# Attention and top-80 expert routing on one core: the expert lists in exact bf16 parts, list one-hots on VectorE, two thirds of the band masks off TensorE, one PSUM ring of four

## The chip, the cores and the metric

The program runs on one core of a Trainium2 chip. The metric is the device time of one execution in microseconds (us). Engines are named as in the profile: PE is TensorE (PEld its weight loads), DVE VectorE, ACT ScalarE, POOL GpSimd, SP SyncE; SP and POOL also issue the DMAs.

## The reference

For 8 batches and 8 heads, 32 global and 512 local tokens of 64 dimensions attend: global tokens to everything, local tokens to the 32 global keys and to a band of 32 positions to either side. The 4608 rows of 512 that come out go through a gate with eight experts, of which each keeps the 80 tokens with the largest gate weight.

```python
s_g = scale * q_g @ k_all.T;  out_g = softmax(s_g) @ v_all
s_ll = where(abs(i - j) <= 32, scale * q_l @ k_l.T, -1e9)
out_l = softmax(concat([scale * q_l @ k_g.T, s_ll])) @ concat([v_g, v_l])
x = concat([out_g, out_l])                       # rows of 512
logits = x @ w_gate;  expert = argmax(logits);  gate_w = softmax(logits)[expert]
for e in range(8):                               # capacity 80
    tok = the 80 tokens of expert e with the largest gate_w
    out[tok] = gate_w[tok] * (relu(x[tok] @ w1[e]) @ w2[e])
```

## The kernel before

The main loop has 16 stages, s = 0 to 15, one for each half of a batch's heads (four heads, k = 0 to 3, in two pairs j). A stage computes on PE: `G_val(s)` and `L_val(s, k)`, which multiply the exponentials of the scores (`eG`, `eL`) by the values (`vgb` global, `vt` local) into `o_ps`; `S_glob(s+1)` and `S_loc(s+1, j)`, the scores of the next stage, whose exponentials ACT takes; `T_tile`, the transposes of queries and keys to come; `X_turn`, which turns the normalised output `xn` for the gate; and `O_glob`, the global queries. In `S_loc` the band mask is made in one of two ways for each head, by the table `MASKER`: "pe" adds a matrix of large negative numbers by one more matmul before the scores (L264, 128x512, bf16), "dve" or "pool" multiplies the exponentials by 0 or 1 afterwards (L277).

In `G_val` every head has 32 rows of the array: four matmuls of 32 rows and 65 columns for each quarter u of the tokens. An fp32 matmul stands in the profile as two records (80 of L473 for 8 batches of 5 matmuls).

After a batch's second stage `gate_pieces(b)` hands a list of small steps to a queue, `bgq`. The loop pops ten of them in each stage, by calls `bg(1)`, `bg(1)`, `bg(1)`, `bg(1)`, `bg(1)`, `bg(2)`, `bg(3)` between the attention's parts. Each engine runs its instructions in the order in which the program is written (the schedule is manual). The steps of a batch are

- `p_xg`, `p_lgT`, `p_lg`, `p_arg`: logits (first by four groups of 512 tokens, then turned back by eight-column matmuls with `sel`, L379), argmax one-hot `oh` and gate weight;
- `p_parts`, `p_turn0`, `p_vi`, `p_turn1`, `p_glob`, five `p_rank`: the gate weight is split into three bf16 parts on POOL; matmuls and VectorE counts (L457) give each token's rank in its expert, by comparison with all tokens of its batch;
- `p_oh`, `p_list`: five one-hots `ohs` of the ranks on POOL (L466) and five fp32 matmuls (L473) put the first 80 values and ids of the batch into `B_ps`; the batch's list is merged with the list so far, `Rl`;
- for batches 1 to 6 `p_diag`, two `p_cmp`, `p_oh2`, `p_sort`: the merged list `M` is sorted again. POOL spreads the values on a diagonal, four fp32 matmuls of 320 columns (L494, L496) make all differences, DVE compares and counts, POOL makes eight one-hots (L506), eight fp32 matmuls (L512) permute.

That is 16 steps for batches 0 and 7 and 21 for batches 1 to 6, against 20 that two stages pop. What is left when the loop ends is run by `bg(100)`; then the indices `idx` are made, the tokens gathered (POOL, indirect DMA), and the eight experts run, each with a scatter to the output from POOL. The weights of experts 6 and 7 are loaded only after the first gathers.

PSUM: `psT` tiles come from a ring T of two banks, `psS` tiles (scores) from a ring S of two, `o_ps` from two double banks.

## Time and profile before

| | |
|---|---|
| runs | 435.69, 431.42, 428.17 us, median 431.42 |
| profiled execution | 427.29 us, its span 425.5 us |
| busy in the span | PE 323.1 us (76%), DVE 160.3 (38%), ACT 116.5 (27%), POOL 159.3 (37%) |
| granted TensorE clock | 0.755 of 2.4 GHz over the span |
| DMA | 51.35 MB, software queue 38.1% and hardware queue 19.5% of the engines' span |

A profile row gives line, engine, operation, output<-inputs, shapes and count, then busy us and the mean ns of one, then the idle time of the engine before it and what released it. The granted clock is given in the windows as PEclk (1.00 is 2.4 GHz, 0.50 is 1.2 GHz).

### The profile page before, as it was taken

The page shows a single profiled execution, that of the slowest core. Times are in us where ns is not written, and L with a number is a line of the kernel's source. Part 1 is how long each engine was busy: PE and PEld are TensorE (multiplying, and loading weights), DVE is VectorE, ACT ScalarE, POOL GpSimd, SP SyncE. Part 2 cuts the span into 40 slices and gives each one's busy share as a digit, 9 for nine tenths or more (in the row PEclk, how much of TensorE's full clock was granted, in tenths as well). Part 3 has the DMA queues.
Part 4 walks back from the last instruction along what each step waited for, and adds up shares of the span by engine and source line. Part 5 has one row for each costly group of instructions (what it writes and reads, how often), then busy time and mean ns, then how long its engine had stood idle before and what let it go on. Part 6 is the DMA issues. An engine that isn't in the chain of part 4 may idle for free. (4 is left out here: it accounts for less than half of the span.)

```text
span 425.5 us, 10554 instructions
## 1 busy us (share of the span) xinstructions
PE 323.1 (76%) x4528; PEld 223.3 (52%) x4528; DVE 160.3 (38%) x422; ACT 116.5 (27%) x181; POOL 159.3 (37%) x301
## 2 busy tenths in 40 slices
...
GB/s 153 176 224 91 198 240 225 166 99 161 160 29 103 161 164 126 28 169 157 102 24 104 101 75 151 100 101 61 193 2 146 53 201 0 2 148 216 127 46 46
DMA packets 61790, 51.35 MB, mean 121 GB/s; under 512 B 45360, under 2 KB 45488, under 8 KB 61744
## 3 DMA queue, kind: packets, MB, share of 16 engines
q0 software_dynamic: 18000, 27.66, 38.1%
q1 hardware_dynamic: 43744, 23.03, 19.5%
...
q14 instruction: 11, 0.09, 0.1%
...
## 5 line engine op out<-in xcount | busy, mean ns | idle before, releaser
L298 PE MATMUL o_ps<-vt,eL 128*64 128x65 f32 x1024 | 53.7, 266 | 0.0
L115 ACT COPY qkT<-T_ps 128x1024 f16<-128x1024 f16 x29 | 29.3, 1011 | 73.9 <-PE T_ps L230 71.2
L298 PEld LDWEIGHTS o_ps<-vt,eL 128*64 128x64 f32 x1024 | 44.9, 173 | 8.5 <-issue 5.4
L342 POOL CAST xb<-xn 128x1024 bf16<-128x1024 f32 x16 | 16.6, 1035 | 74.0 <-DVE xn L305 62.1
L274 ACT ACTIVATE eL<-l_ps 128x512 f32<-128x512 f32 x64 | 34.8, 596 | 31.0 <-PE l_ps L269 30.7
L230 PE MATMUL T_ps<-ident,qk 128*64 128x128 f16 x512 | 26.8, 268 | 16.2 <-DMA qk<-in_q_l_dram 9.5
L506 POOL TENSOR_SCALAR oh<-second,rs 80x80 f32<-80x80 bf16 x48 | 22.1, 473 | 40.1 <-DVE rs L501 32.6
L457 DVE SCALAR_TENSOR_TENSOR junk<-r_ps,gate,second 128x512 bf16<-128x512 f32 x40 | 29.9, 747 | 13.5 <-PE r_ps L456 12.4
L230 PEld LDWEIGHTS <-qk 128*64 128x64 f16 x512 | 22.8, 144 | 20.0 <-DMA qk<-in_q_l_dram 9.5
L466 POOL TENSOR_SCALAR ohs<-second,rank 128x80 f32<-128x80 bf16 x40 | 19.0, 484 | 34.7 <-DVE rank L464 34.7
L289 PE MATMUL o_ps<-vgb,eG 32*128 32x65 f32 x512 | 27.5, 367 | 0.0
L289 PEld LDWEIGHTS o_ps<-vgb,eG 32*128 32x128 f32 x512 | 24.8, 274 | 4.2 <-issue 4.1
L473 PE MATMUL B_ps<-vi,ohs 128*80 128x24 f32 (+1 forms) x80 | 16.9, 299 | 12.7 <-POOL ohs L466 11.6
L337 PE MATMUL x_ps<-identf,xn 128*128 128x128 f32 x128 | 25.3, 331 | 0.5 <-DVE junk L457 0.5
L250 ACT ACTIVATE eG<-G_ps 128x512 f32<-128x512 f32 x16 | 9.5, 596 | 59.0 <-PE G_ps L248 59.0
L473 PEld LDWEIGHTS B_ps<-vi,ohs 128*80 128x80 f32 (+1 forms) x80 | 12.6, 213 | 20.2 <-POOL ohs L466 17.6
L305 DVE TENSOR_TENSOR xn<-o_ps,rec 128x512 f32<-128x512 f32 x32 | 22.1, 692 | 2.1
L277 DVE TENSOR_TENSOR eL<-eL,first 128x512 f32<-128x512 f32 x16 | 11.1, 692 | 31.3 <-ACT eL L274 31.3
L115 DVE COPY xT<-x_ps 128x512 f32<-128x512 f32 x32 | 21.9, 683 | 1.4 <-PE x_ps L337 1.2
...
L456 PE MATMUL r_ps<-S3T,oh3T 24*128 24x512 bf16 x40 | 17.7, 442 | 5.0 <-DVE junk L457 2.1
L264 PE MATMUL l_ps<-first 128*128 128x512 bf16 x48 | 18.5, 440 | 1.8 <-ACT eG L250 1.1
...
## 6 DMA issues: line engine op xcount, KB each, us to landing
...
```

Source lines behind the costliest of these rows:

```text
L115: (nc.scalar.copy if eng is nc.scalar else eng.tensor_copy)(out=out, in_=in_)
L230: nc.tensor.transpose(out=T_ps[64 * q:64 * q + 64, i, :], in_=qk16[b % 2][:, t, q, 8 * half + i, :], identity=ident16[:, :])
L264: mm(out=l_ps[hh][:], lhsT=identb, rhs=neg, start=True, stop=False, skip_group_check=True)
L274: nc.scalar.activation(out=e, in_=l_ps[hh][:], func=AF.Exp, scale=scale)
L289: mm(out=oview(s, k)[:, u, :], lhsT=eG[s % 2][r, 128 * u:128 * u + 128], rhs=vgb[r, s // 2, s % 2, :], start=(u == 0), stop=False, skip_gr ...
L298: mm(out=o[64 * odd:64 * odd + 64, u, :], lhsT=eL[s % 2][:, k, 64 * t:64 * t + 64], rhs=v[:, 4 * odd + u, k, :], start=False, stop=(u == 3 ...
L305: nc.vector.tensor_tensor(out=xn[:, s % 2, :, j].rearrange("p u h d -> p h u d"), in0=o[:, :, :, 0:64], in1=rec[:].unsqueeze(3).to_broadca ...
L337: nc.tensor.transpose(out=x_ps[:, 128 * u:128 * u + 128], in_=xn[:, s % 2, u, j].rearrange("p h d -> p (h d)"), identity=identf[:, :])
L457: nc.vector.scalar_tensor_tensor(out=junk[:], in0=ps_[:], scalar=st["gate"][:, u:u + 1], in1=wst[:, 512 - 128 * u:1024 - 128 * u], op0=ALU ...
L466: nc.gpsimd.tensor_scalar(out=ohs[:, u, :], in0=nat if b == 0 else rev, scalar1=rank[:, u:u + 1], scalar2=None, op0=ALU.is_equal)
L473: mm(out=B_ps[:].rearrange("r e c -> r (e c)"), lhsT=ohs[0:n, u, :], rhs=st["vi"][0:n, u].rearrange("p e c -> p (e c)"), start=(u == 0), s ...
L506: nc.gpsimd.tensor_scalar(out=oh2[:, e, :], in0=nat[0:cap], scalar1=st["rs"][:, e:e + 1], scalar2=None, op0=ALU.is_equal)
```

## The change

- `MASKER` goes from pe, pe, pe, dve to pool, pe, dve, pool: one mask matmul a stage in place of three, and two multiplications on POOL, one on DVE.
- `G_val`: the global values `vgb` are laid out with the two heads of a pair block-diagonally, so that one matmul of 64 rows and 130 columns does what two of 32 rows and 65 columns did.
- Logits by token quarters: sixteen matmuls of 128 columns that add up the four head groups in PSUM, and one fp32 transpose in place of the four `sel` matmuls. ACT's copy is 128x128 instead of 128x512.
- The value is carried as three bf16 parts and each id as two, seven columns `vi` in place of three in fp32. The matmuls of `p_list`, `p_cmp` and `p_sort` become bf16: 5 of 56 columns, 24 of 80, 8 of 7. `p_diag` is gone, so the list has 20 steps for batches 1 to 6.
- `ohs` and `oh2` are made by one DVE instruction each, the comparison by eight DVE counts (L495 after), the `oh3` copy moves to ACT, and so does the copy of `X_turn(s, 1)`.
- `psT` and `psS` share one ring of four banks.
- `vgb` is cleared in parts at the start (eight memsets on DVE, one before), the `cid` load is part of `second`.

```diff
-MASKER = ["pe", "pe", "pe", "dve"]
+MASKER = ["pool", "pe", "dve", "pool"]
...
     def psT(shape, dt, name):
-        return ps.tile(shape, dt, tag="T", bufs=2, name=name)
+        return ps.tile(shape, dt, tag="S", bufs=4, name=name)
 
     def psS(name):
-        return ps.tile([P, 512], FP32, tag="S", bufs=2, name=name)
+        return psT([P, 512], FP32, name)
...
-    vgb = cp.tile([P, B, 2, 65], FP32, name="vgb")
+    vgb = cp.tile([P, B, 2, 2, 65], FP32, name="vgb")
...
-    ohs = cp.tile([P, 5, cap], FP32, name="ohs")
+    lgT = cp.tile([P, P], FP32, name="lgT")
+    Rl = cp.tile([cap, 8, 7], BF16, name="Rl")
+    Rv = cp.tile([cap, 8], FP32, name="Rv")
+    oh2 = cp.tile([cap, 8, cap], BF16, name="oh2")
+    ohs = cp.tile([P, 5, cap], BF16, name="ohs")
...
-    def oview(s, k):
-        return ost[s][k // 2][:, k % 2, 0:260].rearrange("p (u d) -> p u d", u=4)
+    def oview(s, k, u):
+        c = 130 * (u % 2) + 65 * (k % 2)
+        return ost[s][k // 2][:, u // 2, c:c + 65]
 
     def G_val(s):
         ost[s] = [psO(f"o_ps{s}_{j}") for j in range(2)]
         for u in range(4):
-            for k in range(4):
-                r = slice(32 * k, 32 * k + 32)
-                mm(out=oview(s, k)[:, u, :], lhsT=eG[s % 2][r, 128 * u:128 * u + 128],
-                   rhs=vgb[r, s // 2, s % 2, :], start=(u == 0), stop=False, skip_group_check=True)
+            for j in range(2):
+                r = slice(64 * j, 64 * j + 64)
+                c = 130 * (u % 2)
+                mm(out=ost[s][j][:, u // 2, c:c + 130], lhsT=eG[s % 2][r, 128 * u:128 * u + 128],
+                   rhs=vgb[r, s // 2, s % 2].rearrange("p h d -> p (h d)"), start=(u % 2 == 0), stop=False,
+                   skip_group_check=True)
...
         def p_lgT():
-            ps_ = psT([P, 512], FP32, f"lgT_ps{b}")
+            ps_ = psT([P, P], FP32, f"lgT_ps{b}")
             for f in range(4):
-                mm(out=ps_[32 * f:32 * f + 32, :], lhsT=wg[:, f, :], rhs=xslot(2 * b + f // 2, f % 2)[:],
-                   start=True, stop=True, skip_group_check=True)
+                for c in range(4):
+                    mm(out=ps_[32 * c:32 * c + 32, :], lhsT=wg[:, f, :],
+                       rhs=xslot(2 * b + f // 2, f % 2)[:, 128 * c:128 * c + 128],
+                       start=(f == 0), stop=(f == 3), skip_group_check=True)
             nc.scalar.copy(out=lgT[:], in_=ps_[:])
 
         def p_lg():
-            lg = psT([P, 5, E], FP32, f"lg{b}")
-            for u in range(4):
-                mm(out=lg[:, u, :], lhsT=lgT[:, 128 * u:128 * u + 128], rhs=sel[:], start=(u == 0), stop=False,
-                   skip_group_check=True)
-            mm(out=lg[:, 4, :], lhsT=identb, rhs=zb[:], start=False, stop=False, skip_group_check=True)
+            lg_ps = psT([P, 5, 32], FP32, f"lg{b}")
+            lg = lg_ps[:, :, 0:8]
+            nc.tensor.transpose(out=lg_ps[:, 0:4, :].rearrange("p u e -> p (u e)"), in_=lgT[:], identity=identf[:, :])
+            mm(out=lg[:, 4, :], lhsT=identb, rhs=zb[:], start=True, stop=False, skip_group_check=True)
...
+            nc.vector.tensor_tensor(out=t("sc", [P, 5, E])[:], in0=st["oh"][:],
+                                    in1=st["gate"][:].unsqueeze(2).to_broadcast([P, 5, E]), op=ALU.mult)
+            nc.scalar.copy(out=t("oh3", [P, 5, 3, E], BF16)[:], in_=st["oh"][:].unsqueeze(2).to_broadcast([P, 5, 3, E]))
...
         def p_vi():
-            oh, g, vi = st["oh"], nc.gpsimd, st["vi"]
-            g.tensor_copy(out=vi[:, :, :, 0], in_=st["sc"][:])
-            for c in range(2):
-                g.tensor_tensor(out=vi[:, :, :, 1 + c], in0=oh[:],
-                                in1=cid[:, b, :, c].unsqueeze(2).to_broadcast([P, 5, E]), op=ALU.mult)
+            nc.gpsimd.tensor_tensor(out=st["vi"][:, :, 3:7, :], in0=st["oh"][:].unsqueeze(2).to_broadcast([P, 5, 4, E]),
+                                    in1=cid[:, b].unsqueeze(3).to_broadcast([P, 5, 4, E]), op=ALU.mult)
...
         def p_oh():
             rank = t("rank", [P, 5])
             nc.vector.tensor_tensor(out=rank[:], in0=st["rk1"][:], in1=st["rk2"][:], op=ALU.add)
-            for u in range(5):
-                nc.gpsimd.tensor_scalar(out=ohs[:, u, :], in0=nat if b == 0 else rev, scalar1=rank[:, u:u + 1],
-                                        scalar2=None, op0=ALU.is_equal)
+            nc.vector.tensor_tensor(out=ohs[:], in0=(nat if b == 0 else rev).unsqueeze(1).to_broadcast([P, 5, cap]),
+                                    in1=rank[:].unsqueeze(2).to_broadcast([P, 5, cap]), op=ALU.is_equal)
 
         def p_list():
-            B_ps = psT([cap, 8, 3], FP32, f"B_ps{b}")
+            B_ps = psT([cap, 8, 7], FP32, f"B_ps{b}")
             for u in range(5):
                 n = P if u < 4 else SG
-                mm(out=B_ps[:].rearrange("r e c -> r (e c)"), lhsT=ohs[0:n, u, :],
-                   rhs=st["vi"][0:n, u].rearrange("p e c -> p (e c)"), start=(u == 0), stop=(u == 4))
+                mm(out=B_ps[:], lhsT=ohs[0:n, u, :], rhs=st["vi"][0:n, u].rearrange("p c e -> p e c"),
...
+            M = t("M", [cap, 8, 7], BF16)
+            bv = t("bv", [cap, 8])
+            mv = t("mv", [cap, 8])
+            mask = t("mask", [cap, 8, 7], U8)
+            nc.scalar.copy(out=M[:], in_=B_ps[:])
+            nc.vector.tensor_reduce(out=bv[:], in_=B_ps[:, :, 0:3], axis=AX.X, op=ALU.add)
+            nc.vector.tensor_tensor(out=mask[:], in0=Rv[:].unsqueeze(2).to_broadcast([cap, 8, 7]),
+                                    in1=bv[:].unsqueeze(2).to_broadcast([cap, 8, 7]), op=ALU.is_ge)
             nc.vector.copy_predicated(out=M[:], mask=mask[:], data=Rl[:])
...
+            nc.vector.tensor_tensor(out=mv[:], in0=Rv[:], in1=bv[:], op=ALU.max)
+            fin["M"], fin["mv"] = M, mv
 
         def p_cmp(h):
             def f():
-                es = slice(4 * h, 4 * h + 4)
                 D_ps = psT([cap, 4, cap], FP32, f"D_ps{b}_{h}")
-                mm(out=D_ps[:].rearrange("i e k -> i (e k)"), lhsT=negones[:],
-                   rhs=mdiag[:, es].rearrange("k e i -> k (e i)"), start=True, stop=False)
-                mm(out=D_ps[:].rearrange("i e k -> i (e k)"), lhsT=identf[0:cap, 0:cap],
-                   rhs=st["M"][:, es, 0:1].to_broadcast([cap, 4, cap]), start=False, stop=True)
-                nc.vector.tensor_tensor(out=gt2[:, es], in0=D_ps[:],
...
-                if h == 1:
-                    nc.vector.tensor_reduce(out=t("rs", [cap, 8])[:], in_=gt2[:], axis=AX.X, op=ALU.add)
+                if h == 0:
+                    t("rs", [cap, 8])
+                for e in range(4 * h, 4 * h + 4):
+                    for c in range(3):
+                        mm(out=D_ps[:, e % 4, :], lhsT=st["M"][:, e, c:c + 1].to_broadcast([cap, cap]),
+                           rhs=identb[0:cap, 0:cap], start=(e % 4 == 0 and c == 0), stop=(c == 2),
+                           skip_group_check=True)
+                for e in range(4 * h, 4 * h + 4):
+                    nc.vector.scalar_tensor_tensor(out=junk[0:cap, 0:cap], in0=D_ps[:, e % 4, :],
+                                                   scalar=st["mv"][:, e:e + 1], in1=w80, op0=ALU.subtract,
+                                                   op1=ALU.is_gt, accum_out=st["rs"][:, e:e + 1])
...
         def p_oh2():
-            for e in range(8):
-                nc.gpsimd.tensor_scalar(out=oh2[:, e, :], in0=nat[0:cap], scalar1=st["rs"][:, e:e + 1],
-                                        scalar2=None, op0=ALU.is_equal)
+            nc.vector.tensor_tensor(out=oh2[:], in0=nat[0:cap].unsqueeze(1).to_broadcast([cap, 8, cap]),
+                                    in1=st["rs"][:].unsqueeze(2).to_broadcast([cap, 8, cap]), op=ALU.is_equal)
...
         def p_sort():
-            R_ps = psT([cap, 8, 3], FP32, f"R_ps{b}")
+            R_ps = psT([cap, 8, 7], FP32, f"R_ps{b}")
             for e in range(8):
                 mm(out=R_ps[:, e, :], lhsT=oh2[:, e, :], rhs=st["M"][:, e, :], start=(e == 0), stop=(e == 7),
                    skip_group_check=True)
-            nc.vector.tensor_copy(out=Rl[:], in_=R_ps[:])
+            nc.scalar.copy(out=Rl[:], in_=R_ps[:])
+            nc.vector.tensor_reduce(out=Rv[:], in_=R_ps[:, :, 0:3], axis=AX.X, op=ALU.add)
...
-            ls += [p_diag, p_cmp(0), p_cmp(1), p_oh2, p_sort]
+            ls += [p_cmp(0), p_cmp(1), p_oh2, p_sort]
...
+    for k in range(4):
+        r = slice(32 * k, 32 * k + 32)
+        nc.vector.memset(vgb[r, :, :, 1 - k % 2, :], 0.0)
+        nc.vector.memset(vgb[r, :, :, k % 2, 64:65], 1.0)
...
-        X_turn(s, 1, nc.vector)
+        X_turn(s, 1, nc.scalar)
...
-        nc.vector.tensor_scalar(out=idx[:, c, :], in0=M[:, :, 1 + c], scalar1=BIG, scalar2=None, op0=ALU.add)
+        nc.vector.scalar_tensor_tensor(out=idx[:, c, :], in0=M[:, :, 3 + 2 * c], scalar=BIG,
+                                       in1=M[:, :, 4 + 2 * c], op0=ALU.add, op1=ALU.add)
```

The list steps on PE at the end of the last stage, program before: `x_ps_1` is that stage's second `X_turn`, `B_ps`, `D_ps` and `R_ps` belong to batch 6, `xgT_ps` is the first step of batch 7.

```order
L337 MATMUL x_ps_1_4309<-identf,xn 128x128 x4
L456 LDWEIGHTS oh3T
L456 MATMUL r_ps_3_4315<-S3T,oh3T 128x512
...
L456 MATMUL r_ps_4_4318<-S3T,oh3T 128x512
L473 MATMUL B_ps_4338<-vi_4172,ohs 80x24 x5
L494 MATMUL D_ps_0_4350<-mdiag,negones 80x320
L496 MATMUL D_ps_0_4350<-M_4344,identf 80x320
L494 MATMUL D_ps_1_4354<-mdiag,negones 80x320
L496 MATMUL D_ps_1_4354<-M_4344,identf 80x320
L512 MATMUL R_ps_4368<-M_4344,oh_110 80x3 x8
L366 MATMUL xgT_ps_4378<-identf,xgn_4091 128x128
```

The same place on PE now (rows of a tile that follow one another alike are left out):

```order
L450 MATMUL r_ps_4_4282<-S3T,oh3T 128x512
L336 MATMUL x_ps_0_4285<-identf,xn 128x128 x4
L316 MATMUL og_4291<-vt_82,eQ_90 32x65 x16
L321 MATMUL og_4291<-vgb,egg 32x65 x4
L466 LDWEIGHTS ohs
L466 MATMUL B_ps_4319<-vi_4158,ohs 80x56
...
L491 MATMUL D_ps_0_4334<-first,M_4325 80x80
...
L336 MATMUL x_ps_1_4352<-identf,xn 128x128 x4
...
L491 MATMUL D_ps_1_4358<-first,M_4325 80x80
...
L507 MATMUL R_ps_4376<-M_4325,oh_107 80x7
...
L365 MATMUL xgT_ps_4397<-identf,xgn_4153 128x128
```

Before, batch 6's last two rank steps and its whole list stood behind the attention of the last stage; now they are spread over that stage, and batch 7's steps follow its second `X_turn` and the sort.

DVE at the end of a batch's list, program before (batch 6):

```order
L464 TENSOR_TENSOR rank_4321<-rk_4299,rk_4266 128x5
L480 COPY M_4344<-B_ps_4338 80x24
L481 TENSOR_TENSOR mask_4345<-Rl,M_4344 80x24
L483 COPY_PREDICATED M_4344<-mask_4345,Rl 80x24
L498 TENSOR_TENSOR gt_111<-D_ps_0_4350,second 80x320
L498 TENSOR_TENSOR gt_111<-D_ps_1_4354,second 80x320
L501 TENSOR_REDUCE rs_4358<-gt_111 80x8
L514 COPY Rl<-R_ps_4368 80x24
```

And now:

```order
L458 TENSOR_TENSOR rank_4316<-rk_4218,rk_4216 128x5
L459 TENSOR_TENSOR ohs<-second,rank_4316 128x400
L477 TENSOR_REDUCE bv_4326<-B_ps_4319 80x8
L478 TENSOR_TENSOR mask_4328<-Rv,bv_4326 80x56
L480 COPY_PREDICATED M_4325<-mask_4328,Rl 80x56
L481 TENSOR_TENSOR mv_4327<-Rv,bv_4326 80x8
L495 SCALAR_TENSOR_TENSOR junk,rs_4335<-D_ps_0_4334,mv_4327,second 80x80 x4
L495 SCALAR_TENSOR_TENSOR junk,rs_4335<-D_ps_1_4358,mv_4327,second 80x80 x4
L501 TENSOR_TENSOR oh_107<-second,rs_4335 80x640
L510 TENSOR_REDUCE Rv<-R_ps_4376 80x8
```

Both sets of one-hots and the counts stand on DVE now; in the stages that compute scores the mask multiplication of head 2 stands between the two groups of four counts.

## Rows read from the trace of the kernel before

**Rows 1.** Windows: us, busy us of each engine, PEclk, DMA share, GB/s.

```profile
32.20:50.80 18.60, 17.42 (x444) 13.59 (x442) 8.35 (x18) 11.41 (x18) 7.94 (x12) 1.00 0.68 138
50.80:83.80 33.00, 28.29 (x500) 20.41 (x498) 16.09 (x43) 14.37 (x22) 12.90 (x26) 0.84 0.94 213
83.80:295.60 211.80, 182.07 (x2553) 125.78 (x2552) 86.57 (x240) 68.47 (x105) 78.95 (x158) 0.73 0.49 110
295.60:333.60 38.00, 32.35 (x406) 22.48 (x405) 17.56 (x48) 5.66 (x10) 13.30 (x28) 0.68 0.46 99
333.60:348.50 14.90, 10.04 (x34) 6.16 (x35) 2.33 (x6) 0.00 (x0) 8.55 (x16) 0.50 0.84 153
348.50:371.50 23.00, 11.64 (x58) 5.94 (x58) 10.34 (x30) 1.42 (x3) 7.86 (x21) 0.50 0.09 17
371.50:425.50 54.00, 28.81 (x352) 19.49 (x352) 11.76 (x24) 3.50 (x8) 19.68 (x22) 0.82 0.56 115
```

**Rows 2.** Groups by line: busy, mean ns of one, idle before them.

```profile
L274 ACT ACTIVATE eL<-l_ps 128x512 f32<-128x512 f32 x64 | 34.8, 596 | 31.0 <-PE l_ps L269 30.7
L457 DVE SCALAR_TENSOR_TENSOR junk<-r_ps,gate,second 128x512 bf16<-128x512 f32 x40 | 29.9, 747 | 13.5 <-PE r_ps L456 12.4
L264 PE MATMUL l_ps<-first 128*128 128x512 bf16 x48 | 18.5, 440 | 1.8 <-ACT eG L250 1.1 <-ACT eL L274 0.7
L473 PE MATMUL B_ps<-vi,ohs 128*80 128x24 f32 (+1 forms) x80 | 16.9, 299 | 12.7 <-POOL ohs L466 11.6
L512 PE MATMUL R_ps<-M,oh 80*80 80x3 f32 x96 | 14.1, 246 | 5.2 <-POOL oh L506 4.9
L277 DVE TENSOR_TENSOR eL<-eL,first 128x512 f32<-128x512 f32 x16 | 11.1, 692 | 31.3 <-ACT eL L274 31.3
L379 PE MATMUL lg<-sel,lgT 128*128 128x8 f32 x64 | 9.9, 282 | 1.7 <-ACT lgT L374 1.6
L487 POOL TENSOR_TENSOR mdiag<-identf,M 80x640 f32<-80x640 f32 x6 | 7.6, 1265 | 5.1 <-DVE M L483 5.1
L393 DVE SCALAR_TENSOR_TENSOR key<-sh,second 128x40 f32<-128x40 f32 x8 | 1.6, 195 | 0.1
```

**Rows 3.** Timeline of `G_val` at either clock: start, us, instructions.

```profile
41.16 1.12 PE L289 MATMUL o_ps<-vgb,eG 32*128 32x65 f32 x32
...
123.29 1.99 PE L289 MATMUL o_ps<-vgb,eG 32*128 32x65 f32 x32
```

**Rows 4.** Timeline of the sort's differences, matmuls and one weight load.

```profile
118.81 1.35 PE L494 MATMUL D_ps<-mdiag,negones 80*80 80x320 f32 x2
...
119.95 1.27 PE L496 MATMUL D_ps<-M,identf 80*80 80x320 f32 x2
119.95 0.26 PEld L496 LDWEIGHTS D_ps<-M,identf 80*80 80x80 f32 x1 [0.28 <-issue]
```

**Rows 5.** Timeline of the experts' bf16 matmuls of 80 columns, at either clock.

```profile
375.14 1.23 PE L721 MATMUL h_ps<-eQ,wr 128*128 128x80 bf16 x16 [0.42 <-DVE eQ L712]
...
389.95 0.74 PE L721 MATMUL h_ps<-eQ,qk 128*128 128x80 bf16 x16
```

**Rows 6.** Timeline around 60 us: POOL and DVE together, a wait for PSUM.

```profile
60.21 1.04 POOL L342 CAST xb<-xn 128x1024 bf16<-128x1024 f32 x1 [0.40 <-DVE key L393]
...
60.45 0.85 DVE L398 TENSOR_TENSOR oh<-key,m 128x40 f32<-128x40 f32 x1
...
62.26 0.64 PE L230 MATMUL T_ps<-ident,qk 128*64 128x128 f16 x16 [1.74 <-DVE xT L115]
```

**Rows 7.** Timeline of the end of batch 7's list.

```profile
364.59 2.33 POOL L466 TENSOR_SCALAR ohs<-second,rank 128x80 f32<-128x80 bf16 x5 [6.87 <-DVE rank L464]
...
366.87 3.77 POOL L681 MEMSET xT<- 80x512 bf16 x8
367.47 0.18 DVE L480 COPY M<-B_ps 80x24 f32<-80x24 f32 x1 [3.04 <-PE B_ps L473]
...
368.11 2.56 DVE L679 TENSOR_SCALAR idx<-M 80x8 uint32<-80x8 f32 x2
...
371.55 1.10 POOL L684 DMA_INDIRECT xT<-x_scr,idx  x1 [0.91 <-POOL xT L681]
```

96 lines of the change are left out of this document (35 added, 61 removed).

## The prediction, made before the changed kernel ran

> **What bounds the kernel.** I read the windows first, cut by the starts of `G_val`, then the groups by line, then the timeline. In the windows [rows 1] PE is busy 17.4 of 18.6 us in stages 0 and 1, 182 of 211.8 in stages 4 to 13; from stage 2 on no engine but PE and its loads passes 49% (ACT 61% before that; the DMA share is 0.94 in stages 2 and 3, 0.49 afterwards). So PE's static order is the bound of the loop. Two things make a stage pair, 18.6 us without gate steps, into 42.4 us (211.8 / 5): some 9.5 us of gate matmuls and 5 us of waits, and the clock, 1.00 in the first window and 0.73 later, which is 1.2 GHz for (1 - 0.73) / 0.5 = 54% of the time. The same 32 records take 1.12 us at 2.4 GHz and 1.99 at 1.2 [rows 3], a factor of 1.77. Check: (18.6 + 9.5) us of full-clock work at a rate of 0.46 + 0.54 / 1.77 = 0.765 is 36.7, and 5 of waits make 41.7.
>
> After the loop 14.9 and 23.0 us [rows 1], together 37.9, are a chain of small steps: the list of batch 6 left in the queue (21 steps a batch, 20 popped), then all of batch 7. The last 54.0 us (experts, weights 6 and 7, scatters) start with the first gather and are not touched; I take them as they are.
>
> **The sum, part by part.** Per batch, that is per pair of stages, PE time:
>
> - Masks: 32 of the 48 matmuls of L264 go, 18.5 / 48 = 0.385 us each [rows 2], four a pair: -1.5. In their place POOL gets 32 multiplications: 1.265 us for 640 columns [rows 2], so 1.0 for 512, 32 us in all, while it loses 40 + 48 one-hots and the diagonals; DVE keeps its one. The first is wanted by `L_val(s+1, 0)` half a stage later, the other by `L_val(s+1, 3)` later still, so PE hides them. Queued behind them on POOL are `shift_v`, `X_cast` and the DMA issues, each with more than 1 us to spare. If that cover failed, at most 1 us a stage, 16 us in all.
> - Logits: L379 is (9.9 + 1.7) / 8 = 1.45 us a batch [rows 2]; one 128-column transpose, at the 0.28 of one such record, replaces it: -1.2. The sixteen quarter matmuls stream as many columns as the four did: 0.
> - List: L473 is (16.9 + 12.7) / 8 = 3.7 us, paced by POOL's one-hots. Five bf16 matmuls at the pace of L721 (0.74 / 16 = 0.046 us, or 1.23 / 16 = 0.077 [rows 5]) are 0.3. A new wait stands before them: DVE must finish a count (0.75), a copy, `rg`, `xgn`, `rank` and the one-hot (692 x 400 / 512 = 0.54 us [rows 2]), against `X_turn`, `O_glob` and `T_tile` on PE: about 1.2 left. So -2.2.
> - Differences: four fp32 matmuls are eight records at 0.55 us ((119.95 - 118.81) / 2 [rows 4]), 4.4 at 1.2 GHz, half at 2.4, about 3.5 in the mix. Now 24 x 0.046 to 0.077 = 1.1 to 1.85, plus 0.8 for the merged list (an ACT copy, mask, predicated copy) directly behind the list on PE: -1.2.
> - Sort: L512 was (14.1 + 5.2) / 6 = 3.2 us. Now 0.5, and a wait: from the end of the first differences DVE needs four counts, the mask of head 2, four counts and `oh2`. A count of 80 columns lies between 0.20 (40 columns, L393) and 0.75 (512, L457 [rows 2]); I take 0.4 with its accumulator read, near the small one: 1.6 + 0.7 + 1.6 + 692 x 640 / 512 = 0.87, together 4.8, of which `S_loc`, `X_turn` and the second differences on PE cover 1.7. So 0.5 + 3.1: +0.4 (bounds -1 and +3).
> - The ring of four takes away waits like the 1.74 us of `T_ps` on a copy two tiles back [rows 6], and `oh3` comes from ACT instead of a late POOL: -1.5 together (0 to -3). Against it, `X_turn(s, 1)` on ACT stands between two exponentials and the copy that `p_glob` waits for; L274's 0.596 us has its shape [rows 2]: +0.6.
> - `G_val`: eight groups of four records at 0.111 us become eight of two with twice the columns. From below half of that (-0.9 a pair), from above twice (+1.8 at 2.4 GHz). I take +0.5, nearer to zero, because in rows 4 the load of the next weights (0.26 us) fits wholly inside the running matmul of the same rows (0.55).
>
> Sum of a pair: -1.5 - 1.2 - 2.2 - 1.2 + 0.4 - 1.5 + 0.6 + 0.5 = -6.1. Six such pairs (batches 1 to 6) give -36.6, batch 0 (no sort) -5.3, stages 0 and 1 -1.2: -43. The same number of waits in shorter, denser stages should give a little clock back; from 54% at 1.2 GHz to 49% is worth 0.6 us a pair, -4. **Loop: -47.**
>
> **Tail:** the 14.9 us of batch 6's list go, since its 20 steps now end with the loop (its cost is in the pairs). In batch 7's chain the logits save 1.5. The one-hots and list go from 3.0 us (364.5 to 367.4 [rows 7]) to 1.2: -1.8. The indices took 2.56 us for two instructions of 80x8 while POOL's memsets ran, and the gather followed those memsets; without `ohs` in front on POOL they are over before: -2.5. **Tail: -21.**
>
> At nothing: the memsets of `vgb` (about 4 us more on DVE at the start; PE's first work waited until 9.5 us for queries) and the dropped `cid` load, both hidden by loads.
>
> 427.3 - 47 - 21 = **359 us**, against the profiled execution's own 427.3; the median of the runs is 431.4, 1% more, which the range takes in. A kernel like this cannot be told from no change within 2%, 8.6 us.
>
> **A rule against it.** The Trainium skill, "TensorE: Matmul & The Clock Gate", Part 3, says that a weight load overlaps running matmuls only where the row group differs. The new `G_val` has two row groups where it had four, so by that rule load and stream would add up. Rows 4 show the contrary for 80 rows, so I keep +0.5; no row shows 64-row pairs. A second rule, "SBUF — State Buffer", section "Who interferes with whom", says that a DVE instruction with two SBUF inputs and a GpSimd one that reads SBUF lock each other out. By it the 32 masks would hold up the one-hots on DVE.
>
> **Rivals.**
> 1. *`G_val` twice as long.* Load and stream in series: 0.111 us more in 16 x 8 groups is 14 us at 2.4 GHz, 25 at 1.2, 20 in the mix. For it: 130 columns of fp32. Against: rows 4. 377 us.
> 2. *DVE's chain is the new bound of the odd stages.* In rows 6 a DVE instruction took 0.85 us instead of 0.2 while POOL ran a 1.04 us cast. If each of about three such instructions in the list chain loses 0.6 us to a mask, or a count takes 0.65, seven batches lose 2 us: 14. 373 us.
> 3. *The clock recovers.* At 30% of the loop at 1.2 GHz a pair is 23.6 us of work at a rate of 0.87 plus 6 of waits, 33.1 against 35.7, seven times -2.6: 341 us. For it: stages 0 and 1 hold 1.00 with dense work. Against: the waits before list and sort stay, and in the trace the clock fell after such pauses.
> 4. *The loop runs at 1.2 GHz throughout* (slower). The removed masks are the only full-array matmuls of 512 bf16 columns; if what is left with the waits of 3 us doesn't bring the clock up, a pair is 23.6 x 1.77 + 3.5 = 45.3, five 226; batch 0's 42, the last 40, the first two stages 30: 338 against 301.4. 427.3 + 37 - 21 = 443 us. It turns slower from about nine tenths of the loop at 1.2 GHz on: the forecast's loop is 254 at 49%, and 301.4 + 21 = 322 is reached at 0.49 + 0.51 x (322 - 254) / (338 - 254) = 0.90. Against: the window of stages 0 and 1 holds 1.00, with the fp32 value matmuls in it.
> 5. *The change doesn't shorten PE's order*, because loads come late in denser stages: DMA was 0.94 in stages 2 and 3. Then only the tail and the stages from 4 on at half: about 422, no change. Against: 0.49 later.
>
> **Chances and range.** Forecast (345 to 368) 0.48, rival 1 0.12, rival 2 0.16, rival 3 0.13, rival 4 0.05, rival 5 0.06. The range 335 to 390 holds forecast and rivals 1 to 3, up to rival 2 with the upper bound of the sort (373 + 6 x 2.6 = 389). Faster by over 2%: 0.89; within: 0.06; slower: 0.05.
>
> **What would show it.** The changed profile should have L261 with 16 masks; no POOL one-hots; PE idle before the list about 1 us and before `R_ps` about 3; `G_val` near 1.1 us at 2.4 GHz (about 2.0 in rival 1); stage pairs of 34 to 37 us in the middle; PEclk 0.74 to 0.77 (0.85 in rival 3, 0.5 in rival 4); from the loop's end to the first gather 17 us; then again 54. It would be wrong if the last 54 us moved, or if waits that I do not list replaced POOL's.

## The result and the profile after

The changed kernel takes 365.97 us in the median of four runs (359.17 to 368.78), the kernel before 430.67: a ratio of 0.841, with a 95% interval of 0.826 to 0.857. Medians here and below are of all executions, ratios of those within 1.5% of each kernel's fastest. The forecast was 359, with a range of 335 to 390. The profiled execution took 364.19 us, 63.1 less than the one of before.

The windows of the changed kernel, cut at the same places as [rows 1] (starts of `G_val` of stages 0, 2, 4, 14, end of the loop, first gather); the columns are those of [rows 1].

```profile
27.90:44.70 16.80, 16.80 (x408) 13.80 (x406) 7.66 (x16) 10.11 (x16) 9.56 (x12) 0.95 0.63 123
44.70:80.30 35.60, 25.12 (x475) 18.69 (x474) 14.72 (x42) 17.13 (x28) 16.69 (x24) 0.86 1.02 220
80.30:256.30 176.00, 145.14 (x2499) 110.28 (x2498) 92.62 (x315) 75.46 (x130) 74.80 (x107) 0.77 0.60 137
256.30:286.50 30.20, 24.49 (x393) 18.67 (x391) 16.04 (x54) 6.98 (x15) 9.99 (x16) 0.78 0.66 141
286.50:306.60 20.10, 8.77 (x76) 4.96 (x76) 10.44 (x41) 1.80 (x6) 5.09 (x13) 0.50 0.53 104
306.60:362.40 55.80, 30.03 (x352) 20.55 (x352) 11.65 (x24) 3.50 (x8) 19.70 (x22) 0.78 0.54 112
```

Against [rows 1] the five middle pairs went from 211.8 to 176.0 us: PE's busy time fell by 36.9 and its idle time hardly moved (29.7 and 30.9). The stretch behind the loop is 20.1 us for 37.9. The last stretch is the same within 2 us. In the loop only stages 2 and 3 became longer, 35.6 for 33.0.

Stage by stage, in us (the forecast is the sum's, with its 0.6 for the clock in each pair):

| stretch | forecast | measured |
|---|---|---|
| start to first `G_val` | 0 | -4.3 |
| stages 0, 1 | -1.2 | -1.8 |
| stages 2, 3 | -5.9 | +2.6 |
| stages 4 to 13 | -33.5 | -35.8 |
| stages 14, 15 | -6.7 | -7.8 |
| loop's end to first gather | -21 | -17.8 |
| experts | 0 | +1.8 |

The terms show in PE's groups by line. First the kernel before, stages 4 to 13: busy, mean ns of one, idle before them and its releasers.

```profile
L264 PE MATMUL l_ps<-first 128*128 128x512 bf16 x30 | 11.5, 441 | 0.0
L494 PE MATMUL D_ps<-mdiag,negones 80*80 80x320 f32 x16 | 10.7, 771 | 2.0 <-POOL mdiag L487 2.0
L473 PE MATMUL B_ps<-vi,ohs 128*80 128x24 f32 (+1 forms) x48 | 10.2, 303 | 7.6 <-POOL ohs L466 7.0
L496 PE MATMUL D_ps<-M,identf 80*80 80x320 f32 x16 | 9.7, 706 | 0.0
L512 PE MATMUL R_ps<-M,oh 80*80 80x3 f32 x64 | 8.1, 236 | 1.8 <-POOL oh L506 1.8
L379 PE MATMUL lg<-sel,lgT 128*128 128x8 f32 x40 | 5.3, 259 | 0.9 <-ACT lgT L374 0.8
```

The same work in the changed kernel, same stages.

```profile
L491 PE MATMUL D_ps<-first,M 80*80 80x80 bf16 x120 | 8.3, 238 | 5.1 <-DVE M L480 5.0
L261 PE MATMUL l_ps<-first 128*128 128x512 bf16 x10 | 4.1, 411 | 0.0
L466 PE MATMUL B_ps<-vi,ohs 128*80 128x56 bf16 (+1 forms) x25 | 4.0, 284 | 5.3 <-DVE ohs L459 5.3
L507 PE MATMUL R_ps<-M,oh 80*80 80x7 bf16 x40 | 3.5, 210 | 11.7 <-DVE oh L501 11.7
L380 PE MATMUL lg<-identf,lgT 128*128 128x128 f32 x5 | 1.6, 328 | 0.0
L437 PE MATMUL d_ps<-S3T,oh3T 24*128 24x32 bf16 x25 | 1.4, 173 | 5.2 <-ACT S3T L116 5.2
```

The counts say how many batches stand behind a row: by the queue's lag the kernel before makes 4.8 lists (48 records of 10) and four sorts (64 of 16) in these ten stages, the changed one five of each. Busy and idle together, for one batch: list 3.7 us before and 1.9 after, so -1.8 (forecast -2.2); differences 5.1 (L494 and L496 overlap: together they are busy 18.3 us) and 2.7, -2.4 (-1.2); sort 2.5 and 3.0, +0.6 (+0.4). For one pair the masks are -1.5 (-1.5), and the logits, L379 and the four head groups of `lgT_ps` (7.0 us before, 5.4 after), -1.2 (-1.2). The idle time has moved to DVE's results, as forecast: 1.1 us before `B_ps`, 2.3 before `R_ps`.

The chain behind that longest wait, on DVE, once a pair: duration, line, and in brackets what it waited for. Four counts of 0.30 + 0.08 us, head 2's mask, four counts, the one-hots.

```profile
148.73 0.30 DVE L495 SCALAR_TENSOR_TENSOR junk<-D_ps,mv,second 80x80 bf16<-80x80 f32 x1 [0.67 <-PE D_ps L491]
148.96 0.08 DVE L495 DVE_READ_ACCUMULATOR junk<-D_ps,mv,second 80x1 f32 x1
...
149.98 0.68 DVE L274 TENSOR_TENSOR eL<-eL,first 128x512 f32<-128x512 f32 x1
...
152.15 0.82 DVE L501 TENSOR_TENSOR oh<-second,rs 80x640 bf16<-80x640 bf16 x1
```

And PE at the same place, with the `G_val` of stage 2 above it for its duration at 2.4 GHz.

```profile
44.74 1.16 PE L288 MATMUL o_ps<-vgb,eG 64*128 64x130 f32 x16
...
148.04 0.65 PE L491 MATMUL D_ps<-first,M 80*80 80x80 bf16 x12 [1.00 <-DVE M L480]
...
149.74 1.01 PE L491 MATMUL D_ps<-first,M 80*80 80x80 bf16 x12
153.02 0.69 PE L507 MATMUL R_ps<-M,oh 80*80 80x7 bf16 x8 [2.27 <-DVE oh L501]
153.65 2.11 PE L288 MATMUL o_ps<-vgb,eG 64*128 64x130 f32 x16
```

The same twelve differences took 0.65 us and, 1.7 us later, 1.01; `G_val` behind the wait took 2.11 for 1.16. The windows of this stretch show when the granted clock (the third number from the end) fell and came back.

```profile
144.00:149.00 5.00, 2.88 (x82) 2.10 (x70) 3.08 (x13) 1.21 (x2) 1.49 (x3) 1.00 0.67 146
149.00:150.00 1.00, 1.00 (x11) 0.98 (x9) 0.89 (x9) 0.94 (x2) 0.00 (x0) 0.57 1.07 412
150.00:159.00 9.00, 6.73 (x77) 5.46 (x76) 3.17 (x14) 1.97 (x5) 2.88 (x3) 0.50 0.59 135
160.00:165.00 5.00, 5.00 (x143) 3.90 (x137) 2.29 (x9) 3.47 (x6) 2.52 (x4) 1.00 0.02 5
```

It fell just after 149 us, behind waits of 1.12 us (`B_ps`) and 1.00 (`D_ps`) and ahead of the long one; in all five pairs it is already at 1.2 GHz when the long wait begins. It stayed there through the wait and through the next stage's first matmuls, and came back while that stage's `L_val` and `T_tile` ran. What such a stretch costs, the 2.27 us don't show, and the experiments begin there.

### The profile page after: what moved, and what is told of

Same layout as the page of the kernel before. It is cut to its first block, busy times and chain, and to the rows that moved or that the text cites. A ratio compares the mean times of both kernels' runs of the same rounds, so it can differ in the third digit from the quotient of the medians.

```text
span 362.4 us, 10344 instructions
## 1 busy us (share of the span) xinstructions
PE 261.0 (72%) x4384; PEld 195.6 (54%) x4384; DVE 164.1 (45%) x511; ACT 125.9 (35%) x219; POOL 147.3 (41%) x214
## 5 line engine op out<-in xcount | busy, mean ns | idle before, releaser
L274 POOL TENSOR_TENSOR eL<-eL,first 128x512 f32<-128x512 f32 x32 | 38.5, 1204 | 130.3 <-ACT eL L271 110.1
L271 ACT ACTIVATE eL<-l_ps 128x512 f32<-128x512 f32 x64 | 34.6, 594 | 20.4 <-PE l_ps L266 20.1
L227 PE MATMUL T_ps<-ident,qk 128*64 128x128 f16 x512 | 23.8, 249 | 10.1 <-DMA qk<-in_q_l_dram 9.1
L288 PE MATMUL o_ps<-vgb,eG 64*128 64x130 f32 x256 | 29.5, 397 | 0.0
L288 PEld LDWEIGHTS o_ps<-vgb,eG 64*128 64x128 f32 x256 | 25.1, 286 | 2.9 <-issue 2.8
L227 PEld LDWEIGHTS <-qk 128*64 128x64 f16 x512 | 19.7, 130 | 11.7 <-DMA qk<-in_q_l_dram 9.1
L199 ACT COPY vt<-vt 64x1040 f32<-64x1040 f32 x16 | 16.9, 1053 | 9.2 <-DMA vt<-in_v_l_dram 9.0
L733 POOL DMA_INDIRECT out_dram<-xb,idx x8 | 7.4, 926 | 30.5 <-issue 25.3
L274 DVE TENSOR_TENSOR eL<-eL,first 128x512 f32<-128x512 f32 x16 | 11.4, 712 | 18.2 <-ACT eL L271 18.2
L266 PE MATMUL l_ps<-qkT 64*128 64x64 f16 x512 | 14.1, 195 | 5.7 <-DVE xT L116 4.5
L495 DVE SCALAR_TENSOR_TENSOR junk<-D_ps,mv,second 80x80 bf16<-80x80 f32 x48 | 14.2, 297 | 7.7 <-PE D_ps L491 6.2
L336 PEld LDWEIGHTS x_ps<-identf,xn 128*128 128x128 f32 x128 | 15.1, 154 | 3.7 <-issue 1.6
```

The lines of the kernel that those rows point to most:

```text
L199: nc.scalar.copy(out=v[0:64, 4:8], in_=v[64:128, 0:4])
L227: nc.tensor.transpose(out=T_ps[64 * q:64 * q + 64, i, :], in_=qk16[b % 2][:, t, q, 8 * half + i, :], identity=ident16[:, :])
L271: nc.scalar.activation(out=e, in_=l_ps[hh][:], func=AF.Exp, scale=scale)
L274: eng.tensor_tensor(out=e, in0=e, in1=band, op=ALU.mult)
L288: mm(out=ost[s][j][:, u // 2, c:c + 130], lhsT=eG[s % 2][r, 128 * u:128 * u + 128], rhs=vgb[r, s // 2, s % 2].rearrange("p h d -> p (h d)" ...
L336: nc.tensor.transpose(out=x_ps[:, 128 * u:128 * u + 128], in_=xn[:, s % 2, j, u].rearrange("p h d -> p (h d)"), identity=identf[:, :])
```

## The experiments

My theory after the result: PE's order bounds the loop, each term stands for itself, and the granted clock adds a cost to waits that no term had. The rival: the terms count alone, and what a wait is worth is its length. Other rivals stand with the runs. Each kernel was timed beside the kernel before, on the same chip, but not all on one chip, so that two of these kernels are best compared by their ratios (0.01 is 4.3 us). For the stages 4 to 13 of each kernel's profiled execution (the columns are read from the windows and the waits of each):

| kernel | median us | ratio to before, 95% | stages 4 to 13 | PE busy | PE waits | clock |
|---|---|---|---|---|---|---|
| before | 430.7 | 1 | 211.8 | 182.1 | 29.0 | 0.73 |
| changed | 366.0 | 0.841 (0.826 to 0.857) | 176.0 | 145.1 | 30.7 | 0.77 |
| p_sort later | 340.0 | - | 148.4 | 128.3 | 20.0 | 0.90 |
| filler in the wait | 345.7 | 0.799 (0.790 to 0.807) | 161.6 | 136.2 | 25.3 | 0.88 |
| masks undone | 367.1 | 0.845 (0.837 to 0.852) | 177.5 | 143.4 | 34.3 | 0.82 |
| ring undone | 367.5 | 0.847 (0.838 to 0.856) | 175.8 | 136.9 | 38.8 | 0.82 |
| X_turn's copy undone | 354.2 | 0.826 (0.819 to 0.834) | 166.2 | 134.6 | 31.5 | 0.83 |
| G_val undone | 375.9 | 0.876 (0.869 to 0.884) | 177.9 | 146.5 | 31.3 | 0.75 |
| one-hots undone | 382.4 | 0.895 (0.888 to 0.901) | 185.8 | 148.8 | 36.8 | 0.78 |
| three waits moved | 327.0 | 0.755 (0.747 to 0.763) | 142.5 | 125.0 | 17.4 | 0.91 |
| the same, masks undone | 334.3 | 0.772 (0.765 to 0.779) | 148.3 | 132.3 | 15.8 | 0.90 |

**The sort's wait, taken away.** `p_sort` is popped behind the next stage's first `L_val`.

```diff
         L_val(s, 0)
-        bg(1)
+        bg(2 if s % 2 == 0 and s >= 6 else 1)
...
-        bg(3)
+        bg(2 if s % 2 else 3)
```

> The changed kernel with the last step of each list, p_sort, run one step later: behind the first L_val of the next stage instead of at the end of the odd stage. The wait of 2.3 us before R_ps should vanish in five pairs. Theory 1 (a wait is worth its length): -12 us, about 354. Theory 2 (the wait also lowers the granted clock of the G_val and of the work behind it, 2.11 us for 1.16): -16 to -22 us, with the mean clock at 0.82 or more. Rival (DVE's chain is the bound, the wait moves on to another tile): -5 us or less, PE idle before another tile by 1.5 us or more a pair.

Measured: 340.0 us, -26. No interval stands in the table, since its four runs lie too far apart to be compared as one (331.4 to 343.5, at mean clocks of 0.870 to 0.832); but each lies under each of the changed kernel's. The window of the five pairs, and PE's waits in it:

```profile
76.80:225.20 148.40, 128.31 (x2494) 98.82 (x2492) 89.83 (x306) 75.25 (x130) 71.77 (x104) 0.90 0.74 167
```

```profile
PE B_ps L466 <- DVE ohs L459: 6.1, 5, 1.7
PE d_ps L437 <- ACT S3T L116: 5.2, 5, 1.1
PE D_ps L491 <- DVE M L480: 5.0, 5, 1.0
```

The waits fell by 10.7 us, the window by 27.6: the rest, 16.8, is the same work on PE in less time, at a clock of 0.90 for 0.77. Theory 2's mechanism holds, the gain exceeds its range, and no other tile took the wait over. The clock still falls behind `B_ps` and `D_ps`, but comes back sooner: by the clocks of the two windows, some 80 us of the five pairs ran at 1.2 GHz in the changed kernel and some 30 here. Another 4.4 us of difference stand in stages 2 and 3 (31.2 for 35.6), ahead of every sort, and have another cause (the late values, below).

**The sort's wait, filled.** The sharper test takes nothing away: it adds work.

```diff
         def p_sort():
+            dummy = psT([P, 512], FP32, f"dummy{b}")
+            for i in range(4):
+                mm(out=dummy[:], lhsT=identb, rhs=neg, start=True, stop=True)
```

> The changed kernel with work added and none taken away: four mask-like matmuls (128x128 by 512 columns, bf16) into a PSUM tile that nobody reads, ahead of R_ps, where PE waits 2.3 us for DVE's one-hots. They take 1.3 us at 2.4 GHz and 2.2 at 1.2, so they fit into the wait. Theory (what the wait costs beyond its length, 26 us measured for 12 us of waits, is the granted clock that falls around it): faster, -5 to -15 us, about 355, the mean clock at 0.82 or more, though PE does more. Rival A (time follows PE's work and waits alone): 0 to +4 us. Rival B (the late p_sort gained by something else, such as ACT's copies or the PSUM ring): 0.

Measured: 345.7 us, -20 (-18 by the ratios, more than the theory's -15) with 24 more matmuls (three of its runs 343 to 346 at mean clocks of 0.85 to 0.87, one 371 at 0.76). PE at the same place as above:

```profile
141.36 1.01 PE L491 MATMUL D_ps<-first,M 80*80 80x80 bf16 x12
142.17 0.63 PE L507 MATMUL dummy<-first 128*128 128x512 bf16 x1
142.98 0.60 PE L507 MATMUL dummy<-first 128*128 128x512 bf16 x2 [0.18 <-issue]
144.71 0.47 PE L510 MATMUL R_ps<-M,oh 80*80 80x7 bf16 x8 [1.13 <-DVE oh L501]
145.10 1.16 PE L288 MATMUL o_ps<-vgb,eG 64*128 64x130 f32 x16
```

`G_val` behind it takes 1.16 us, not 2.11 (in one of the five pairs still 2.11). DVE is no earlier: from the second differences' start to `R_ps` are 3.35 us, 3.28 in the changed kernel. The five pairs are 14.4 us shorter (161.6 for 176.0), with PE busy 9.0 us less at a clock of 0.88 for 0.77; 3.7 us more were gained in stages 2 and 3, where no filler runs. The clock falls here too (0.51 from 140 to 143 us), but is back at 1.00 from 143 us on, ahead of `G_val`. Neither rival allows a kernel that does more in these stages and is 14 us faster in them: what this wait costs beyond its length lies in the clock. The Trainium skill, "TensorE: Matmul & The Clock Gate", Part 1, section "A second HAM failure mode: psum-queue depth-cycling", tells of a kernel in which short idle times between groups of matmuls, as it went round its PSUM banks, came often enough to make the clock swing. The trace agrees in part: here the clock falls once or twice a pair behind waits of 1.0 to 1.7 us, but these are waits for results of DVE and ACT, not for PSUM banks.

**The masks.** The table `MASKER` as before, first on the changed kernel, then on the one with three waits moved.

```diff
-MASKER = ["pool", "pe", "dve", "pool"]
+MASKER = ["pe", "pe", "pe", "dve"]
```

> The changed kernel with its masks as before: heads 0 to 2 by a mask matmul, head 3 on DVE. Theory (PE's order bounds the loop, so a removed mask matmul is worth its own time): 32 more matmuls of 0.39 us, +12 us, about 378. Rival A (POOL's 32 multiplications hold up DVE's list chain, so taking them away gives most of it back): +4 us or less. Rival B (the mask matmuls keep the granted clock up, and the mean clock rises from 0.79 to 0.83 or more): 0 to -5 us.

Measured: 367.1 us, +1. The row of the five pairs:

```profile
82.80:260.30 177.50, 143.37 (x2519) 105.16 (x2518) 95.21 (x315) 74.73 (x130) 47.03 (x84) 0.82 0.64 141
```

Twenty more mask matmuls, some 8 us, and PE is busy 1.8 us less, at 0.82 for 0.77. Rival B's mechanism explains this (its four runs have mean clocks of 0.81 to 0.84, the changed kernel's 0.78 to 0.80), though there was no gain; rival A's doesn't, since PE's waits for DVE gained nothing (`R_ps` 11.4 us for 11.7, `B_ps` 6.9 for 5.3). Where the clock is high already, the same edit should cost its time:

> The kernel with three of the four waits moved (327 us) and the masks as before the change: 32 more mask matmuls on PE, none on POOL. Undone on the changed kernel itself, this cost about 0 for the 12 us of PE work, with the mean clock rising from 0.79 to 0.83. Theory (there the granted clock gave the 12 us back; here it is 0.86 to 0.91 already and has less to give): +7 to +12 us, about 336. Rival (a mask on POOL or DVE costs the loop as much as one on PE, by late exponentials or a slower DVE): 0 to +3 us.

Measured: 334.3 us against 327.0, +7.3 (the same by the ratios), and the two intervals are apart. In the five pairs PE is busy 7.3 us more, 1.5 a pair, as the sum had it. On the changed kernel the traces show that price given back by the clock. The times alone don't: there the cost is 1.4 us by the ratios, known to some 7 us either way, which excludes the theory's 12 but not 7.3.

**The ring of four.**

```diff
-        return ps.tile(shape, dt, tag="S", bufs=4, name=name)
+        return ps.tile(shape, dt, tag="T", bufs=2, name=name)
...
-        return psT([P, 512], FP32, name)
+        return ps.tile([P, 512], FP32, tag="S", bufs=2, name=name)
```

> The changed kernel with two PSUM rings of two again. Theory: the waits for a copy two tiles back return, 1.5 us a pair of stages as in the sum, +10 us, about 376; PE shows idle time before T_ps, r_ps or og. Rival (the other edits have taken these waits away already, the ring of four does nothing): 0 to +3 us.

Measured: 367.5 us, +1.5. The waits came back, `T_ps` and `og` first:

```profile
PE R_ps L507 <- DVE oh L501: 11.4, 5, 2.3
PE T_ps L227 <- DVE xT L116: 8.7, 5, 1.7
PE D_ps L491 <- DVE M L480: 5.0, 5, 1.0
PE d_ps L437 <- ACT S3T L116: 4.4, 5, 1.0
PE og L316 <- DVE junk L451: 4.2, 5, 0.8
```

They are 8.1 us more in five pairs, 1.6 a pair, as the sum had it; the window is no longer, because PE's work ran at 0.82. Here more waits go with a higher clock. So not every wait lowers it, and why these didn't stays open. In one thing the ring shows plainly: the first `G_val` starts at 31.8 us without it, at 27.9 with it and at 32.2 before, which is the start's -4.3. But stages 2 and 3 win back without it what the start loses (31.7 us for 35.6): the wait of 7.4 us in stage 2, below, isn't there.

**The copy of the second `X_turn`**, back on DVE.

```diff
-        X_turn(s, 1, nc.scalar)
+        X_turn(s, 1, nc.vector)
```

> The changed kernel with the copy of the second X_turn on DVE again. My sum (ACT is late with the copies that p_glob and S_loc wait for, 0.6 us a pair): -5 us. Rival (DVE is the engine that the list and the sort wait for; one more copy of 0.68 us on it in each stage delays the counts): +3 to +6 us, the wait before R_ps growing from 2.3 to about 3.0 us.

Measured: 354.2 us, -12 by the medians and -6.5 by the ratios, whose intervals overlap, so that by them even the sign isn't clear of noise; it is the sum's (the move to ACT costs), not the rival's. The wait of `d_ps` for ACT fell from 5.2 to 3.7 us, that of `R_ps` grew from 11.7 to 13.0, the clock rose to 0.83. In the two traces the five pairs are 9.8 us shorter, 2.0 a pair for the sum's 0.6, and that is PE's busy time (134.6 for 145.1), not the length of waits.

**`G_val` in 32-row matmuls.**

```diff
-                mm(out=ost[s][j][:, u // 2, c:c + 130], lhsT=eG[s % 2][r, 128 * u:128 * u + 128],
-                   rhs=vgb[r, s // 2, s % 2].rearrange("p h d -> p (h d)"), ...)
+                mm(out=oview(s, k, u), lhsT=eG[s % 2][r, 128 * u:128 * u + 128],
+                   rhs=vgb[r, s // 2, s % 2, k % 2], ...)
```

> The changed kernel with G_val in matmuls of 32 rows and 65 columns again, four for each quarter. My sum (+0.5 us a pair for the 64-row form): -4 us, about 362. Rival 1 of the prediction (load and stream in series in the 64-row form, twice the time): -14 to -20 us; the records of the 64-row form in the changed profile (1.16 us at 2.4 GHz, 2.11 at 1.2, for 1.12 and 1.99) speak against it. Rival 2 (no difference): -1 to +1 us.

Measured: 375.9 us, +10 (+15 by the ratios); no reading had that sign. At a given clock the 64-row form costs what the records say, 1.16 for 1.12 us [rows 3] and 2.11 for 1.99, some 0.2 us a pair. Undone, the five pairs are 1.9 us longer, while stages 2 and 3 take 44.5 us for 35.6, with PE waiting 9.9 us (7.4 in the changed kernel) at one place and a clock of 0.65 there (0.86): 6.5 of these 8.9 us are PE's busy time. The wait is that of the late values, below; why the clock is lower, 0.75 over the whole run for 0.79, stays open.

**The one-hots' place.** Both sets on POOL, one instruction each, still in bf16.

```diff
-            nc.vector.tensor_tensor(out=ohs[:], in0=(nat if b == 0 else rev)..., op=ALU.is_equal)
+            for u in range(5):
+                nc.gpsimd.tensor_scalar(out=ohs[:, u, :], in0=nat if b == 0 else rev, scalar1=rank[:, u:u + 1],
+                                        scalar2=None, op0=ALU.is_equal)
```

(and `oh2` likewise, eight.)

> The changed kernel with both sets of one-hots on POOL again, one instruction for each (0.47 us), but in bf16 and for the bf16 matmuls. Theory (PE waits for the end of the one-hots, so their time counts in full): five take 2.3 us for 0.57, eight take 3.7 for 0.82, so 8 x 1.8 + 6 x 2.9 = +32 us, about 398, most of the gain of the list and the sort. Rival (the gain lies in the bf16 matmuls, the place of the one-hots matters little): +8 us or less.

Measured: 382.4 us, +16 (+23 by the ratios). The wait before `B_ps` is 9.6 us for 5.3 and that before `R_ps` 13.5 for 11.7: PE starts with the first one-hot and waits for each, so that the matmuls run between them and the time doesn't count in full. The theory had the direction right, but PE doesn't wait for the last one-hot before it starts, and 32 was too much; the rival's 8 was too little. No run undid the bf16 matmuls alone.

**The queue's lag alone**, on the kernel before: 21 steps a pair.

```diff
-        bg(3)
+        bg(4 if s % 2 else 3)
```

> The kernel before with 21 steps popped in each pair of stages instead of 20, so that no list is left when the loop ends. My sum's reading (the 14.9 us behind the loop are a loss of their own): -13 to -15 us. Rival (these steps cost PE time wherever they run; in the loop only their waits are covered): -3 to -8 us, with the window behind the loop 14 us shorter and the last pair of stages 7 to 11 us longer.

Measured: a ratio of 1.0045 (0.994 to 1.015), no gain; both readings fell. In its profiled execution (444.96 us, the longest of its four) the stretch behind the loop is 23.0 us for 37.9 and the last pair 45.9 for 38.0, as the rival had it. But the five middle pairs take 231.0 for 211.8: PE is busy 196.4 for 182.1, at a clock of 0.70 for 0.73, and its waits are 2.7 us longer in all (that of `R_ps` for POOL's one-hots 10.1 us for 1.8). How much of this the edit does, one such execution can't tell. The runs show that moving these steps into the loop gains nothing by itself; that the change gained by it because it made the steps cheap and one fewer is likely, but not shown.

**The late values.** In stage 2 of the changed kernel PE waits 7.4 us, which makes stages 2 and 3 longer than before. PE and ACT there:

```profile
53.30 0.64 PE L245 MATMUL G_ps<-qkT,kbd 128*64 128x512 f16 x2 [7.40 <-ACT qkT L116]
```

```profile
51.29 1.06 ACT L199 COPY vt<-vt 64x1040 f32<-64x1040 f32 x1 [9.05 <-DMA vt<-in_v_l_dram]
52.25 1.00 ACT L116 COPY qkT<-T_ps 128x1024 f16<-128x1024 f16 x1
```

ACT waits for the values of stage 3, and the copy of `T_ps`, which PE needs, stands behind that wait. I took the other loads for the cause.

```diff
-        if s >= 1 and wq:
+        if s >= 4 and wq:
...
-        zeros(1)
+        zeros(0 if s < 4 else 2 if s < 8 else 1)
```

> The changed kernel with the zero fills of the output and the expert weights loaded from stage 4 on instead of from stages 0 and 1, so that only queries, keys and values are loaded early. Theory (the 7.4 us that PE waits in stage 2 are values that land late behind these loads: rival 5 of the prediction, for one stage): stages 2 and 3 fall from 35.6 to 28 us, -7 us in all, about 358. Rival (the same bytes are late later, or the end waits for the weights): 0, with a wait of PE for a copy of ACT in stages 4 to 8, or a later first scatter.

Measured: 359.2 us, -7 by the medians, with intervals that overlap; but the wait is still there, 6.7 us, and stages 2 and 3 take 34.9, so the theory fell whatever the total. SP's queue in this kernel:

```profile
25.86 3.34 SPq L542 DMA_DIRECT2D second<-csecond  x1
29.32 1.80 SPq L547 DMA_DIRECT2D wg<-in_moe_w_gate_dram  x2
31.16 6.85 SPq L552 DMA_DIRECT2D wgq<-in_moe_w_gate_dram  x8
38.05 13.05 SPq L193 DMA_DIRECT2D vt<-in_v_l_dram  x12
```

SP issues `second`, `wg` and eight small `wgq` loads for 12 us before the values' turn. From 30 to 40 us the DMA share is 0.35, from 40 to 50 it is 1.06, with queries and keys beside the values. But the kernel before has the same loads in the same order on SP, and PE doesn't wait there. What differs is when POOL issues the next queries and keys. The four value loads in question and the queries, before and then changed:

```profile
41.16 2.60 SPq L196 DMA_DIRECT2D vt<-in_v_l_dram  x4
41.65 0.72 POOL L188 DMA_DIRECT2D qk<-in_q_l_dram  x1
...
41.14 9.65 SPq L193 DMA_DIRECT2D vt<-in_v_l_dram  x4
39.33 0.76 POOL L185 DMA_DIRECT2D qk<-in_q_l_dram  x1
```

Before, the queries come 0.5 us behind the values, whose issue takes 2.6 us. The changed loop gets there earlier, the queries are 1.8 us ahead, and the values' issue takes 9.7. The other traces of the changed kernel and its versions agree: with queries issued between 36.6 and 39.6 us PE waits 2.9 to 9.9 us in stage 2 (9.9 with `G_val` undone, at 38.4), with queries at 40.0 and 40.4 (p_sort later, filler) 0.6 and 1.2, at 42.7 (ring undone) not at all. So the values lose a race against queries and keys, and stand behind SP's small loads in it. No run changed that order alone, and moving `wgq` behind the values was not tried.

**Three waits moved.** The late `p_sort`, the first differences behind `S_loc`, and `p_glob` behind the odd stage's first `L_val`.

```diff
         L_val(s, 0)
-        bg(1)
+        bg(3 if s % 2 else (2 if s >= 6 else 1))
...
-        bg(2)
+        bg(1 if s % 2 else 2)
         if nx:
             S_loc(s + 1, 1)
+        if s % 2:
+            bg(1)
         X_turn(s, 1, nc.scalar)
-        bg(3)
+        bg(2 if s % 2 else 1)
```

> The changed kernel with three of the four waits moved behind other PE work: p_sort behind the next stage's first L_val, the differences of the first four heads behind S_loc, and p_glob of the even stage behind the odd stage's first L_val. Theory: the waits of 2.3, 1.05 and 0.35 us a pair go, -12 -8 -2 = -22 us, and -30 if the granted clock rises with it (0.83 or more). Rival (DVE becomes the bound: the rank counts start later, and the wait before B_ps grows by what the wait of p_glob lost): -12 us, with over 2 us idle before B_ps.

Measured: 327.0 us, -39 to the changed kernel (-37 by the ratios, more than the theory's -30), -13 to the one with `p_sort` alone. Of the waits 17.4 us are left in five pairs; that before `B_ps` grew to 8.3, 1.7 a pair, as the rival had it, without deciding.

With the X_turn copy on DVE and the late fills besides:

> The kernel with three of the four waits moved (327 us), the second X_turn's copy on DVE and the fills and weights from stage 4 on. Theory: -7 us from the loads and -3 from the copy (its wait of 0.3 us a pair before p_glob is gone with p_glob's move, so less than the 12 measured on the changed kernel), about 317. Rival (DVE, with the longest chain before B_ps, pays 0.7 us a stage for the copy): 325 or more.

Measured: 326.3 us, a ratio of 0.747 (0.736 to 0.758), not to be told from 0.755; the theory's -10 would be 0.732, so it fell. The five pairs take 142.6 us for 142.5: with the waits moved, the copy's place no longer matters there. The rival has the total right, but the delay on DVE that it named is not seen (the wait before `B_ps` is 8.3 us in both). Stages 2 and 3 are 2.5 us shorter (32.5 for 35.0). Either version is a quarter faster than the kernel before and 11% faster than the changed one.

## Why the prediction was right, and where it was not

- **The bound.** PE's order, as said: of the 35.8 us that the five pairs lost, 36.9 are PE's busy time and the idle time stayed.
- **Masks, logits, list, sort.** Forecast -1.5, -1.2, -2.2, +0.4; the trace has -1.5, -1.2, -1.8, +0.6. Each was sized from one row, and a row was enough. Logits, list and sort were not undone alone, so their prices rest on the rows.
- **Differences.** -2.4 a batch for -1.2. I took the eight fp32 records at a mix of both clocks, 3.5 us; they ran at 1.2 GHz nearly throughout, 18.3 us of busy time in four batches, and had 0.5 us of wait before them. (The record's 0.55 us is 0.57 by the row that it was read from.)
- **Five batches' savings were taken from ten stages that held four sorts.** 7.6 us (5.1 and 2.5) of what the sum credits to these stages stood in the kernel before behind the loop, where the tail credits them again; the larger gain of the differences, 5 x 1.2 = 6.0, made up for most of it.
- **Ring and `X_turn`.** The waits of `T_ps`, `r_ps`, `og`, `S3T_ps` and `oh3T_ps` fell by 15.8 us in five pairs, 3.2 a pair for 1.5; those of `d_ps` and `l_ps` grew by 1.4 a pair for 0.6. The net of -1.8 for -0.9 is near.
- **`G_val`.** +0.3 a pair for +0.5, no doubling: rival 1 (377) is out by its records, 1.16 us for 1.12. The rule cited against the term was not read rightly either: the new matmuls alternate between the two halves of the rows, as the old ones went round four quarters, so the next matmul's weights go to other rows in both.
- **The step that failed: that the terms add up, with 0.6 us a pair for the clock.** The clock is no small term at the end but a factor on all of PE's work, and it answers to where a wait stands. Undone one by one, masks and ring (12 and 10 us in the sum) cost 1 to 2 us each, `X_turn`'s copy gives 2.0 us a pair in the trace for 0.6, and one wait of 2.3 us, 11.7 in the five pairs, is worth 27.6 there. The forecast of 0.74 to 0.77 for the clock came true in these stages (0.77; 0.79 over the span), and the change left as much idle time as it found; whether that is the reason, as the sum had it, no run shows. Rival 3 (341, a clock of 0.85) comes near the kernel with the sort's wait gone (340.0, the five pairs at 0.90).
- **Rival 2.** DVE's chain kept its pace: counts of 0.38 us with their read for an assumed 0.4, one-hots of 0.57 and 0.82 for 0.54 and 0.87. The stretching exists, elsewhere. `sc`, two inputs in SBUF, takes 0.20 us alone and 0.58 in seven of eight cases, when it ends with POOL's cast:

```profile
164.83 1.04 POOL L341 CAST xb<-xn 128x1024 bf16<-128x1024 f32 x1
...
165.34 0.58 DVE L403 TENSOR_TENSOR sc<-oh,gate 128x40 f32<-128x40 f32 x1
```

  The counts, with one input in PSUM, take 0.30 us beside POOL's masks as without them, and no one-hots ran beside a mask or the cast of `xb`. Five of the 14 met POOL's short cast of `xgb`: four kept their 0.82 us (beside one of them it was the cast that took 0.74 us for 0.31), one took 0.67 for 0.57. The Trainium skill, "SBUF — State Buffer", section "Who interferes with whom", gives the rule (a DVE instruction with two SBUF inputs and a GpSimd instruction that reads SBUF lock each other out), and the trace agrees; what rival 2 had wrong is which instructions meet.
- **Stages 2 and 3** were called cheaper by 5.9 and are 2.6 longer. That is rival 5 in one stage. No term of the sum asked what the earlier start would do to the order of the loads on SP's and POOL's queues.
- **The tail.** -17.8 for -21. The indices take 0.25 us for 2.56, as said; but batch 6's sort still stands at its front, with its wait of 2.3, which I had put wholly into the loop.
- **Rival 4 and "no change"** needed a clock of 0.5 or loads that bind; from stage 4 on neither is in the windows. Rival 5's 422 us doesn't follow from its own terms: the tail's -21 alone makes 406.

That the total came within 2% owes something to luck, since the errors partly cancelled: +8.5 us in stages 2 and 3, +3.2 in the tail and +1.8 in the experts against -4.3 at the start and -4.0 in the other stages.
